# Decayed attention and a Mish layer on one core: state products on quarters of the array, q loaded in runs of eight tokens, two-chunk products

## The chip, the core and the metric

The kernel runs on one core of a Trainium2 chip. A core has five engines that run side by side, each through its own list of instructions in order: PE (TensorE, the 128 x 128 matmul array; its weight loads are shown apart as PEld), DVE (VectorE), ACT (ScalarE), POOL (GpSimd) and SP (SyncE, here a sender of DMAs). Matmul results land in PSUM, which has eight banks of 128 partitions x 512 float32. The metric is the device time of one execution in microseconds (us).

## The reference

```python
# q, k, v: (4 batches, 8 heads, 768 tokens, 64) float32; lam: (8,)
for b in range(nb):                                   # blocks of 64 tokens
    intra = einsum('bhic,bhjc->bhij', qb, kb) * Dmask # lam ** distance, causal
    intra = einsum('bhij,bhjd->bhid', intra, vb)
    inter = einsum('bhid,bhde->bhie', qb * lam_pow, kv_state)
    out[:, :, sl] = intra + inter
    kv_state = lam_block * kv_state + einsum('bhsd,bhse->bhde', kb * rev_pow, vb)
x = out.transpose(0, 2, 1, 3).reshape(3072, 512)
h = x @ w_in                                          # (512, 2048)
g = h * tanh(softplus(h))                             # Mish
return g @ w_out                                      # (2048, 512), float32
```

## The kernel before

Tokens are worked in chunks of 128; a *group* n (0 to 5) is chunk n of all four batches b. All matmuls take float16. For each (group, batch) the kernel takes these steps, each named by a short word:

- `lk`, `lq`, `lv` (L152) load k, q, v from GpSimd's DMA queue, casting to float16, into tiles [token, head, 64]. One contiguous piece is one head of one token, so a load is 1,024 pieces of 256 bytes. k and q of (0,0) come as float32 over the queues of SP and ACT (`fk`, `fq`) and are cast by ACT (`ck`) and VectorE (`cq`, L311).
- Turning: k and q must lie with the 64 channels on the partitions. For groups 0 and 1, PE turns them against the identity (`pk`, `pq`, L316) into a float16 bank; VectorE (`kk`, `eq`) or ACT (`ek`, `ea`, L347) copies the bank to SBUF. For groups 2 to 5 the DMA turns them (`tk`, `tq`). Two heads share the 128 partitions (a pair j of four).
- `sc` (L379): the scores of each head, 8 matmuls on half of the array's rows (64 rows x 128 columns), the two heads of a pair in two banks. `mk` (L385): decay and mask, VectorE, two instructions.
- `yo`, `yt` (L396): scores by v, 8 matmuls of 128 rows x 64 columns. `yi` (L410): the state by q, added in the same bank, 4 matmuls of the full array; the state of a pair is a 128 x 128 tile with the two heads' 64 x 64 parts on the diagonal and zeros beside them. `xd` (L415): VectorE scales the sum into x.
- `kp` (GpSimd) or `kd` (VectorE, L351): decayed k. `pv` (L421): decayed k by v, 4 matmuls of the full array (the off-diagonal parts are computed too). `ra` (L427 for group 0, L430): VectorE adds the old state; `wu` (GpSimd, L434) or `wd` (VectorE, L438) multiplies by the decay `lbm`, which is zero off the diagonal.

Then the Mish layer. The first rows of work go as direct products: `u` (L595), 16 matmuls of 128 columns for 512 hidden units of one chunk, and `mu` (L603), Mish by ACT. They cover all of group 0 and half of group 1. All else uses a scheme of seven half-size products for eight: `p` (L558), 4 matmuls of 256 columns, with sums by VectorE (`ws`, `wt`, `ts`, `gs`, `ad`, `c2`; L455, L458) and copies and Mish by ACT (`ca`, `cc`, `m`; L565, L570, L587). The second layer is the same scheme: `o` (L636), 8 matmuls of 256 columns, copies `oa`, `oc`, `e`, `ed`, and stores `st`.

The order of all this is written out by hand as one string, `ORDER`: a step's name, its numbers (group, batch, ...) and behind `@` its PSUM banks. Each engine meets its instructions in the order of this string; an instruction waits until its operands are there and its bank or tile is free. `zz.N` (L296) are N products of zeros by zeros, 128 columns each, whose result is never read; before the change there are 56 in all, all ahead of the first scores.

Of the kernel before, what the change touches and what calls it, by code (L numbers as in the profile page):

```python
# [7 lines left out]
F32 = mybir.dt.float32  # L8
# [7 lines left out]
fk lq.0.1 ir lk.0.1 lk.0.2 lq.0.2 lv.0.0 lv.0.2 lk.1.2 lq.0.3 lv.0.1 lk.0.3 lk.1.0 la ll z0 zz.23@0 pl@1 an ik  # L16
ak fq ck dk di zz.12@0 pq.0.1@2 eq.0.1 zz.10@0 pk.0.1@3 ie kk.0.1 dv.1 zz.11@0 sc.0.1@2,3 mk.0.1.1 pk.0.2@4
pk.0.0@5 wi.1 wi.0 lv.0.3 lq.1.1 kp.0.0 pq.0.2@6 dv.0 kd.0.1 kk.0.0 mk.0.1.0 dp lz kk.0.2 dq kd.0.2 kp.0.3
lq.1.2 lq.1.0 lk.1.1 wi.3 cq ea.0.2 al pq.0.0@6 ea.0.0 ai lm sc.0.2@5,4 mk.0.2.0 mk.0.2.1 yo.0.1@7 sc.0.0@6,1
pv.0.1@3 pk.1.0@2 pq.0.3@5 ek.1.0 ea.0.3 mk.0.0.0 pk.0.3@4 ek.0.3 yo.0.2@6 pv.0.2@2 mk.0.0.1 xd.0.1 xd.0.2  # L20
yo.0.0@1 pk.1.2@5 sc.0.3@4,7 xd.0.0 mk.0.3.0 mk.0.3.1 pv.0.0@6 u.0.1.2@1 ra.0.2 ra.0.1 u.0.1.1@4 u.0.0.0@7
yo.0.3@2 u.0.0.2@3 mu.0.0.2 mu.0.0.0 xd.0.3 ra.0.0 mu.0.1.2 mu.0.1.1 u.0.0.1@2 u.0.0.3@6 pv.0.3@3 ra.0.3
mu.0.0.3 kk.1.2 mu.0.0.1 u.0.1.3@7 mu.0.1.3 wi.2 kd.1.2 lk.1.3 lq.1.3 pq.1.0@1 pk.1.1@4 pq.1.2@5 pq.1.1@6
lv.1.1 kk.1.1 lv.1.0 lv.1.2 ea.1.0 ea.1.1 eq.1.2 u.0.1.0@3 mu.0.1.0 sc.1.0@4,1 sc.1.2@5,6 sc.1.1@2,7 mk.1.0.0
mk.1.1.0 mk.1.1.1 ws.1.1 mk.1.0.1 mk.1.2.0 kd.1.1 mk.1.2.1 u.0.3.0@3 u.0.3.1@4 u.0.3.2@2 mu.0.3.0 mu.0.3.1
u.0.2.0@7 u.0.3.3@3 u.0.2.2@4 pk.1.3@1 pq.1.3@5 mu.0.2.0 mu.0.3.3 mu.0.2.2 mu.0.3.2 u.0.2.1@7 eq.1.3 kk.1.3
ws.2.1 pv.1.1@5 ra.1.1 lv.1.3 sc.1.3@1,6 yt.1.1@3 yt.1.0@4 u.0.2.3@2 yi.1.1 yi.1.0 yt.1.2@5 mk.1.3.0 mk.1.3.1
# [24 lines left out]
mk.3.1.0 mk.3.1.1 gs.2.1.2.4 gs.2.1.4.6 gs.2.1.6.8 ra.3.0 ra.3.1 gs.2.2.0.2 gs.2.2.4.6 gs.2.2.6.8 p.2.3.4
# [49 lines left out]
def kernel(  # L102
# [10 lines left out]
    nc = tc.nc  # L113
# [661 lines left out]
```

## Time and profile before

| | us |
|---|---|
| median of 3 runs (lowest, highest) | 202.05 (200.88, 228.25) |
| the profiled execution | 202.03 |
| its span, first to last instruction | 200.3 |
| PE busy, PE weight loads | 187.9, 165.5 |
| VectorE busy | 163.4 |
| ACT busy, GpSimd busy | 93.4, 94.4 |
| mean granted PE clock | 0.972 |

The busy times belong to the profiled execution, and so do all rows shown below. A row of groups has line, engine, operation, output <- inputs, shapes and count, then the busy time and the mean in ns, then the idle time ahead of them and what ended it. The chain of waits is read from the end of the execution back: each piece is start, length, engine and line.

### The profile page before, as it was taken

The page shows a single profiled execution, that of the slowest core. Times are in us where ns is not written, and L with a number is a line of the kernel's source. Part 1 is how long each engine was busy: PE and PEld are TensorE (multiplying, and loading weights), DVE is VectorE, ACT ScalarE, POOL GpSimd, SP SyncE. Part 2 cuts the span into 40 slices and gives each one's busy share as a digit, 9 for nine tenths or more (in the row PEclk, how much of TensorE's full clock was granted, in tenths as well). Part 3 has the DMA queues.
Part 4 walks back from the last instruction along what each step waited for, and adds up shares of the span by engine and source line. Part 5 has one row for each costly group of instructions (what it writes and reads, how often), then busy time and mean ns, then how long its engine had stood idle before and what let it go on. Part 6 is the DMA issues. An engine that isn't in the chain of part 4 may idle for free.

```text
span 200.3 us, 5347 instructions
## 1 busy us (share of the span) xinstructions
PE 187.9 (94%) x2226; PEld 165.5 (83%) x2226; DVE 163.4 (82%) x307; ACT 93.4 (47%) x172; POOL 94.4 (47%) x105
## 2 busy tenths in 40 slices
PE   8607999999999999999999999999999999999992
PEld 7406899999899888888888998888988888888882
DVE  2797848799999999999999897879858997788611
ACT  3026166418626231068933448721676526873221
POOL 7999675830518670009994099970094000000000
PEclk9965899999999999999999999999999999999998
DMA  6999999999998949345899646999979331000324
GB/s 82 160 157 206 163 198 163 205 202 157 117 121 107 139 36 236 85 95 50 124 159 152 121 93 150 139 154 195 119 128 85 109 104 54 5 0 0 108 95 167
DMA packets 103226, 24.73 MB, mean 123 GB/s; under 512 B 92834, under 2 KB 103202, under 8 KB 103202
## 3 DMA queue, kind: packets, MB, share of 16 engines
q0 software_dynamic: 77024, 13.37, 85.3%
q1 hardware_dynamic: 24992, 10.69, 24.4%
q10 hardware_dynamic: 1186, 0.33, 0.8%
q8 instruction: 17, 0.28, 0.5%
q14 instruction: 7, 0.06, 0.1%
HBM read 27.26 MB, written 6.29 MB: 168 GB/s over the span
## 4 chain that ended last, share of the span: by engine, by line
PE 86%; DVE 7%; DMA 2%; ACT 2%; issue 1%; POOL 1%; POOLq 0%; DVEq 0%
PE b L636 37%; PE b L558 26%; PE b L595 9%; PE b L396 4%; PE b L379 4%; PE b L410 2%; PE b L421 2%; DMA kn<-in_k_dram 2%; PE b L316 2%; DVE qn L311 1%; ACT hsg L603 1%; DVE ws L458 1%; DVE sb L385 1%; DVE dv L260 1%; DVE ktil L351 1%
## 5 line engine op out<-in xcount | busy, mean ns | idle before, releaser
L636 PEld LDWEIGHTS <-hs 128*128 128x128 f16 x384 | 36.9, 98 | 4.5
L636 PE MATMUL b<-wt,hs 128*128 128x256 f16 x288 | 36.5, 273 | 0.0
L587 ACT ACTIVATE hsg<-b 128x512 f16<-128x512 f32 x54 | 30.0, 598 | 11.6 <-PE b L558 10.5
L385 DVE TENSOR_TENSOR sb<-b,dv 128x512 f16<-128x512 f32 x48 | 30.9, 683 | 3.3 <-PE b L379 2.0
L558 PEld LDWEIGHTS <-ws 128*128 128x128 f16 x288 | 27.7, 98 | 3.6 <-DVE ws L458 0.4
L636 PEld LDWEIGHTS <-hsg 128*128 128x128 f16 x288 | 27.7, 98 | 3.5
L558 PE MATMUL b<-xs,ws 128*128 128x256 f16 x216 | 29.3, 273 | 0.0
L434 POOL TENSOR_TENSOR w<-raw,lbm 128x512 f16<-128x512 f32 x9 | 12.0, 1347 | 32.8 <-DVE raw L430 32.8
L636 PE MATMUL b<-wout,hsg 128*128 128x256 f16 x192 | 24.9, 273 | 0.0
L595 PE MATMUL b<-xt,win 128*128 128x128 f16 x384 | 23.8, 219 | 0.0
L558 PEld LDWEIGHTS <-win 128*128 128x128 f16 x216 | 20.7, 98 | 2.7 <-issue 0.3
L152 POOL DMA_DIRECT2D qn<-in_q_dram x23 | 21.3, 933 | 2.9 <-DMA wout<-in_moe_w_out_dram 1.4
L595 PEld LDWEIGHTS <-win 128*128 128x128 f16 x384 | 22.1, 98 | 0.4
L152 POOL DMA_DIRECT2D kn<-in_k_dram x23 | 20.8, 926 | 3.3 <-DMA wout<-in_moe_w_out_dram 1.7
L351 POOL TENSOR_TENSOR ktil<-kn,lkt 128x512 f16<-128x512 f16 x13 | 14.7, 1137 | 14.9 <-DMA kn<-in_k_dram 14.9
L152 POOL DMA_DIRECT2D vn<-in_v_dram x24 | 21.7, 917 | 0.0
L558 PE MATMUL b<-xt,win 128*128 128x256 f16 x144 | 20.5, 273 | 0.0
L603 ACT ACTIVATE hsg<-b 128x512 f16<-128x512 f32 x24 | 13.3, 604 | 12.9 <-PE b L595 12.9
L565 ACT ACTIVATE b<-b 128x512 f32<-128x512 f32 x18 | 10.5, 590 | 17.9 <-PE b L558 17.2
L415 DVE TENSOR_TENSOR xt<-b,lqi 128x512 f16<-128x512 f32 x24 | 15.8, 686 | 3.2 <-PE b L396 1.7
L455 DVE TENSOR_TENSOR c<-b,p 128x512 f32<-128x512 f32 x18 | 12.3, 685 | 4.2 <-PE b L558 4.2
L455 DVE TENSOR_TENSOR b<-b,p 128x512 f32<-128x512 f32 x18 | 12.5, 697 | 3.4 <-PE b L558 1.7
(77 smaller groups left out, 282.7 us busy)
## 6 DMA issues: line engine op xcount, KB each, us to landing
out_dram<-osb SPq DMA_DIRECT2D x23, 256.0 KB, 2.5
vn<-in_v_dram POOLq DMA_DIRECT2D x24, 128.0 KB, 6.0
qn<-in_q_dram POOLq DMA_DIRECT2D x23, 128.0 KB, 5.8
kn<-in_k_dram POOLq DMA_DIRECT2D x23, 128.0 KB, 5.8
win<-in_moe_w_in_dram POOLq DMA_DIRECT2D x4, 512.0 KB, 9.5
wout<-in_moe_w_out_dram POOLq DMA_DIRECT2D x4, 512.0 KB, 10.4
osb<-in_k_dram SPq DMA_DIRECT2D x1, 256.0 KB, 3.0
osb<-in_q_dram ACTq DMA_DIRECT2D x1, 256.0 KB, 5.5
```

The costliest lines, as they stand in the source:

```text
L152: nc.gpsimd.dma_start(out=to[n, b], in_=rows(t, n, b))
L351: engine.tensor_tensor(out=ktil[n, b], in0=kn[n, b], in1=bc(lkt, 2, D), op=ALU.mult)
L385: nc.vector.tensor_tensor(out=sb[n, b, t], in0=pS[n, b][t], in1=dv[:, t], op=ALU.mult)
L415: nc.vector.tensor_tensor(out=xts(n, b), in0=pO.pop((n, b)), in1=lqi, op=ALU.mult)
L434: nc.gpsimd.tensor_tensor(out=wst[b], in0=raw.pop((n, b)), in1=lbm, op=ALU.mult)
L455: nc.vector.tensor_tensor(out=o, in0=a, in1=b, op=ALU.add)
L558: nc.tensor.matmul(t[:, mi, :], w_half(i, s, mi, kc), x_half(n, i, kc), start=(i in (1, 5) and mi == 0 and kc == 0), stop=(mi == 1 and kc ...
L565: nc.scalar.activation(ph[n, s, "b"], ph[n, s, "a"], AF.Copy)
L587: nc.scalar.activation(hidden(n, col - 1, row - 1)[:, 2 * s : 2 * s + 2], src, AF.Mish)
L595: nc.tensor.matmul(ph[n, w, b][:, f, :], win[:, kc, ni * 128 : (ni + 1) * 128], xt[n][:, kc, b * C : (b + 1) * C], start=(f == 0 and kc == ...
L603: nc.scalar.activation(hidden(n, b // 2, w // 2)[:, f : f + 4, cols], ph.pop((n, w, b)), AF.Mish)
L636: nc.tensor.matmul(t[:, tb, :], g_half(n, i, ki, tb), o_half(i, ki), start=(i in (1, 5) and tb == 0 and ki == 0), stop=(tb == 1 and ki == ...
```

## The change

1. **State on quarters.** The state of a pair is now 128 x 64: the two heads' 64 x 64 parts one below the other, without zeros. `pv` becomes 8 matmuls of 128 rows x 64 columns with 64 moving columns; `yi` becomes 8 matmuls on the diagonal quarters (64 x 64) of the array; `ra`, `wu`, `wd` work on 128 x 256 elements instead of 128 x 512. `sc` also goes on quarters: 16 matmuls of 64 x 64 instead of 8 of 64 x 128. The step `lz` (clearing `lbm`) goes.
2. **q of groups 0 and 1 in runs of 8 tokens.** A partition holds 8 tokens of one head, so a load is 128 pieces of 2 KB. PE turns it by 16 matmuls against parts of the identity (64 columns each) into a float32 bank, and the copy to SBUF puts the tokens back in order.
3. **Two-chunk products.** 20 of the 24 `u` steps become `uu`: 8 matmuls of 256 columns for 256 hidden units of two chunks; 20 `mu` become `mv`.
4. **Wide zero products.** `zz` takes 512 columns per matmul; the counts are now 12, 20, 5, 124, 2 and 2 in units of 128 columns (165 in all).
5. **Tiles and order.** Eight instead of seven buffers each for k, q and v. The whole `ORDER` is new: among other things three more k are copied by ACT and not by VectorE (`ek` 5, `kk` 3), five more k are decayed by GpSimd (`kp` 18, `kd` 2), q is copied by ACT seven times and once by VectorE, 14 loads (of groups 0 and 1) stand ahead of the first slice of w_in instead of 11 ahead of its slices 1 and 0, and steps of like shape stand in groups (three or four `sc`, four `yi`).

```diff
 ORDER = """
-fk lq.0.1 ir lk.0.1 lk.0.2 lq.0.2 lv.0.0 lv.0.2 lk.1.2 lq.0.3 lv.0.1 lk.0.3 lk.1.0 la ll z0 zz.23@0 pl@1 an ik
-ak fq ck dk di zz.12@0 pq.0.1@2 eq.0.1 zz.10@0 pk.0.1@3 ie kk.0.1 dv.1 zz.11@0 sc.0.1@2,3 mk.0.1.1 pk.0.2@4
...
+fk ir lk.0.1 lq.1.2 lq.0.2 lk.0.2 lv.0.1 lk.0.3 lk.1.0 lq.1.3 lq.0.3 lq.1.0 lq.0.1 lk.1.2 lv.0.0 lq.1.1 ll fq
+la ck z0 zz.12@0 pl@1 ik di cq dk zz.20@0 pk.0.0@2 zz.5@0 pq.0.0@3 pk.0.1@4 zz.124@0 pq.0.1@5 an ek.0.1 ak
+kd.0.2 kk.0.0 dv.0 dp eq.0.0 ie dq dv.1 sc.0.0@1,4 mk.0.0.0 ai ea.0.1 al wi.0 lv.0.2 mk.0.0.1 pk.1.0@2
+pk.0.2@3 pk.0.3@6 ek.1.0 ek.0.3 sc.0.1@5,7 ek.0.2 mk.0.1.1 mk.0.1.0 pq.0.3@1 pq.0.2@4 pq.1.3@2 yo.0.0@6 xd.0.0
+ea.0.3 ea.0.2 pk.1.2@7 ek.1.2 zz.2@0 yo.0.1@3 xd.0.1 pq.1.0@5 pq.1.1@1 ea.1.0 sc.0.3@6,4 zz.2@0 sc.0.2@3,7
+ea.1.1 uu.0.0.0.0@5 mk.0.2.0 uu.0.0.0.1@1 mk.0.3.1 mk.0.2.1 mk.0.3.0 lv.0.3 wi.2 wi.3 lk.1.1 lk.1.3 lv.1.0
+kp.0.0 wi.1 pv.0.0@3 yo.0.2@4 pq.1.2@7 lm ea.1.3 mv.0.0.0.0 mv.0.0.0.1 ea.1.2 xd.0.2 pv.0.2@2 yo.0.3@6
...
+    def runs(t, n, b):
+        return t[b, :, n * C : (n + 1) * C, :].rearrange("h (g r) c -> h g r c", r=RUN)
...
     def lq(n, b):
-        load(qn, q, "qn", n, b)
+        if n > 1:
+            load(qn, q, "qn", n, b)
+            return
+        qn[n, b] = work.tile([128, H, D], F16, name="qn", tag="qn", bufs=8)
+        nc.gpsimd.dma_start(out=qn[n, b], in_=runs(q, n, b))
...
-        t = bank(at, [128, 4 * C])
-        for _ in range(m):
-            nc.tensor.matmul(t[:, 0:128], kzero, kzero, start=True, stop=True)
+        t = bank(at, [128, 4, C])
+        for n in [4] * (m // 4) + [1] * (m % 4):
+            nc.tensor.matmul(t[:, 0:n], kzero, bc(kzero, 1, n), start=True, stop=True)
...
     def pq_(n, b, at):
-        pq[n, b] = turn_by_pe(qn[n, b], at)
+        o = pq[n, b] = bank(at, [128, RUN, JP, C // RUN])
+        pick = ident.rearrange("p (j t g) -> p t j g", t=2, g=C // RUN)
+        for r in range(RUN):
+            for t in range(2):
+                nc.tensor.matmul(o[part[t], r], qn[n, b][:, r, :], pick[:, t], start=(r == 0), stop=(r == RUN - 1))
+
+    def q_copy(copy, n, b):
+        src = pq.pop((n, b))
+        copy(turned(qraw, "qraw", n, b).rearrange("p j (g r) -> p r j g", r=RUN), src)
...
         for j in range(JP):
-            for t in range(2):
-                nc.tensor.matmul(pS[n, b][t][:, j, :], kraw[n, b][part[t], j, :],
-                                 qraw[n, b][part[t], j, :], start=(j == 0), stop=(j == JP - 1))
+            for x in range(2):
+                for t in range(2):
+                    nc.tensor.matmul(pS[n, b][t][part[x], j, :], kraw[n, b][part[t], j, part[x]],
+                                     qraw[n, b][part[t], j, :], start=(j == 0), stop=(j == JP - 1))
...
     def yi(n, b):
         for j in range(JP):
-            nc.tensor.matmul(pO[n, b][:, j, :], wst[b][:, j, :], qraw[n, b][:, j, :],
-                             start=False, stop=(j == JP - 1), skip_group_check=True)
+            for t in range(2):
+                nc.tensor.matmul(pO[n, b][part[t], j, :], wst[b][part[t], j, :], qraw[n, b][part[t], j, :],
+                                 start=False, stop=(j == JP - 1), skip_group_check=True)
...
     def pv_(n, b, at):
-        o = pv[n, b] = bank(at, [128, JP, C])
+        o = pv[n, b] = bank(at, [128, JP, D])
         for j in range(JP):
-            nc.tensor.matmul(o[:, j, :], flat(ktil[n, b])[:, j * C : (j + 1) * C],
-                             flat(vn[n, b])[:, j * C : (j + 1) * C], start=(j == 0), stop=(j == JP - 1))
+            for t in range(2):
+                nc.tensor.matmul(o[part[t], j, :], ktil[n, b][:, 2 * j + t, :], vn[n, b][:, 2 * j + t, :],
+                                 start=(j == 0), stop=(j == JP - 1))
...
+    def uu(n, w, h, f0, at):
+        ph[n, w, h, f0] = bank(at, [128, 2, HT])
+        for f in range(2):
+            ni = 4 * w + 2 * f0 + f
+            for kc in range(NKC):
+                nc.tensor.matmul(ph[n, w, h, f0][:, f, :], win[:, kc, ni * 128 : (ni + 1) * 128],
+                                 xt[n][:, kc, h * HT : (h + 1) * HT],
+                                 start=(f == 0 and kc == 0), stop=(f == 1 and kc == NKC - 1))
```

More of the change, by code (lines that the diff above doesn't have):

```diff
@@ L150, in load @@
     def load(to, t, name, n, b):
-        to[n, b] = work.tile([128, H, D], F16, name=name, tag=name, bufs=7)
+        to[n, b] = work.tile([128, H, D], F16, name=name, tag=name, bufs=8)
         nc.gpsimd.dma_start(out=to[n, b], in_=rows(t, n, b))
@@ L173, in fq @@
         f32["q"] = work.tile([128, H, D], F32, name="osb", tag="osb", bufs=4)
-        nc.scalar.dma_start(out=f32["q"], in_=rows(q, 0, 0))
+        nc.scalar.dma_start(out=f32["q"], in_=runs(q, 0, 0))
     @step
@@ L202 @@
     lqi = const.tile([128, JP, C], F32, name="lqi")
-    lbm = const.tile([128, JP, C], F32, name="lbm")
+    lbm = const.tile([128, JP, D], F32, name="lbm")
     kzero = const.tile([128, C], F16, name="kzero")
@@ L270, in lz @@
     @step
-    def lz():
-        nc.vector.memset(lbm, 0.0)
-    @step
     def al():
-        for t in range(2):
-            rs = slice(64 * t, 64 * t + 64)
-            nc.scalar.activation(lbm[rs, :, rs], bc(lnp[rs], 2, D), AF.Exp, scale=float(C))
+        nc.scalar.activation(lbm, bc(lnp, 2, D), AF.Exp, scale=float(C))
     @step
@@ L304, in ck @@
     def ck():
-        kn[0, 0] = work.tile([128, H, D], F16, name="kn", tag="kn", bufs=7)
+        kn[0, 0] = work.tile([128, H, D], F16, name="kn", tag="kn", bufs=8)
         nc.scalar.activation(kn[0, 0], f32["k"], AF.Copy)
@@ L309, in cq @@
     def cq():
-        qn[0, 0] = work.tile([128, H, D], F16, name="qn", tag="qn", bufs=7)
+        qn[0, 0] = work.tile([128, H, D], F16, name="qn", tag="qn", bufs=8)
         nc.vector.tensor_copy(qn[0, 0], f32["q"])
+    part = [slice(0, 64), slice(64, 128)]
     def turn_by_pe(src, at):
@@ L342, in eq_ @@
     def eq_(n, b):
-        nc.vector.tensor_copy(turned(qraw, "qraw", n, b), pq.pop((n, b)))
+        q_copy(nc.vector.tensor_copy, n, b)
     @step
     def ea(n, b):
-        nc.scalar.activation(turned(qraw, "qraw", n, b), pq.pop((n, b)), AF.Copy)
+        q_copy(lambda o, x: nc.scalar.activation(o, x, AF.Copy), n, b)
     def decayed(engine, n, b):
@@ L370, in tq @@
         nc.sync.dma_start_transpose(out=turned(qraw, "qraw", n, b), in_=flat(qn[n, b]))
-    part = [slice(0, 64), slice(64, 128)]
     @step
@@ L428, in ra @@
             return
-        raw[n, b] = work.tile([128, JP, C], F32, name="raw", tag="raw", bufs=3)
+        raw[n, b] = work.tile([128, JP, D], F32, name="raw", tag="raw", bufs=3)
         nc.vector.tensor_tensor(out=raw[n, b], in0=pv.pop((n, b)), in1=wst[b], op=ALU.add)
```

154 lines of the change are left out of this document (78 added, 76 removed).

## The prediction, on record before the result

> **What bounds the kernel now.** I read first the busy shares and the slices of the page, then the same busy times over four stretches, which I cut where TensorE's (PE's) work changes its kind.
>
> ```profile
> PE 187.9 (94%) x2226; PEld 165.5 (83%) x2226; DVE 163.4 (82%) x307; ACT 93.4 (47%) x172; POOL 94.4 (47%) x105
> ...
> PEclk9965899999999999999999999999999999999998
> ...
> GB/s 82 160 157 206 163 198 163 205 202 157 117 121 107 139 36 236 85 95 50 124 159 152 121 93 150 139 154 195 119 128 85 109 104 54 5 0 0 108 95 167
> ```
> ```profile
> 0.00:6.00 6.00, 4.63 (x46) 4.24 (x47) 1.12 (x7) 2.39 (x4) 4.86 (x10) 1.00 0.88 88
> 6.00:16.00 10.00, 2.85 (x44) 2.05 (x41) 9.50 (x16) 1.43 (x3) 9.93 (x13) 0.77 2.13 167
> 16.00:22.60 6.60, 6.54 (x80) 4.84 (x81) 4.53 (x9) 4.09 (x6) 5.06 (x6) 0.57 1.69 186
> 22.60:197.00 174.40, 173.85 (x2064) 154.37 (x2061) 148.23 (x278) 85.19 (x158) 74.56 (x78) 1.00 1.05 120
> ```
>
> The columns are the stretch, its length, the busy time of PE, PE's weight loads, DVE (VectorE), ACT (ScalarE) and POOL (GpSimd), the granted clock, DMA share and GB/s. From 22.6 us on PE is busy 173.85 of 174.40 us: there only less PE work helps. Before it PE does 5.6 us of useful work (the turns, scores and states ahead of the first direct product, priced below) in 22.6 us, 6.54 us of its time at a granted clock of 0.57. After the last product at 197 us come 3.3 us of copies and stores. So the end is start of the dense stream + its work + tail, and the change can move the first two. The chain of waits shows what sets the start.
>
> ```profile
> 2.59 4.19 DMA kn<-in_k_dram
> ...
> 13.82 2.19 DVE qn L311
> 16.02 0.05 issue
> 16.06 0.61 PE b L316 x4
> ...
> 20.14 0.57 PE b L396 x8
> ...
> 22.80 2.68 PE b L595 x48
> ```
> ```profile
> PE b L316 <- DVE qn L311: 5.5, 1, 5.5
> ```
>
> VectorE does a row of small constants, then the cast of q (L311), and PE stands still 5.5 us for it. Then all goes at half clock: intra (L396) takes 0.57 us for 8 matmuls, later 0.34 (below).
>
> **The dense stream, term by term.** The same chain prices each kind of matmul at full clock.
>
> ```profile
> 54.40 0.87 PE b L636 x8
> ...
> 57.45 0.22 PE b L421 x4
> 57.68 0.89 PE b L595 x16
> ...
> 72.77 0.33 PE b L379 x8
> 73.10 3.60 PE b L636 x32
> ...
> 76.70 0.34 PE b L396 x8
> 77.04 0.55 PE b L379 x16
> ...
> 77.93 1.75 PE b L636 x16
> ...
> 82.30 0.79 PE b L396 x24
> 83.09 0.55 PE b L410 x8
> ```
>
> A 256-column matmul costs 0.109 us (0.87/8), one of 128 columns 0.0556 (0.89/16), so each further 128 columns 0.0535. Scores (64 rows x 128 columns of the array) cost 0.22 per 8: 0.55 less 0.33. Intra (128 x 64) costs 0.028 per matmul, from (0.79 - 0.34)/16. Both run two at a time. What stays over is a change of the array's shape: 0.33 - 0.22 = 0.11 us going in, and 3.60 - 32 x 0.109 = 0.11 going out.
>
> *Two-chunk products (uu).* 20 of 24 direct steps change from 16 matmuls of 128 columns (0.89) to 8 of 256 (0.87): -0.02 x 20 = **-0.35 us**. They need both chunks of a half, so the first one needs two finished x tiles.
>
> ```profile
> L396 PEld LDWEIGHTS <-vn 128*64 128x64 f16 x192 | 6.2, 115 | 2.3 <-issue 1.2 <-DVE hs L455 0.2 <-DMA win<-in_moe_w_in_dram 0.2
> L421 PEld LDWEIGHTS <-ktil 128*128 128x128 f16 x80 | 5.9, 101 | 0.9 <-issue 0.4
> ```
>
> *State update (pv, 20 steps).* Four matmuls, 0.22, become eight of 64 columns on 128 x 64. By the slope a 64-column matmul costs 0.029, pairs run together as intra does: 4 x 0.029 = 0.12, -0.106 x 20 = **-2.1**. From both sides: nothing gained if the eight weight loads (115 ns each in intra's rows against 98 for full ones) set the pace at 0.028 each, +0.22 x 20 = +4.5 if none pair. I take the row of intra, the nearest.
>
> *Inter (yi, 20 steps) and scores (sc, 24 steps) on quarters.* Inter becomes eight matmuls, two quarters at a time: 4 x 0.056 = 0.22, what four cost now. Scores become sixteen: at four at a time 0.22, as now; at two at a time 0.45, +0.22 x 24 = +5.4. No row has a quarter. Two halves run at once by rows (L379) and by columns (L396), and I take four at once: **0** for both; a gain is excluded, since each quarter still takes 128 columns through the array and no more than four quarters exist. The other end stays a rival.
>
> *Changes of shape.* I counted them in the two written orders: 54 before, 59 after; from the first direct product on, 42 and 46 (pv and inter now differ in shape from the products, but the new order puts pv beside intra and inter beside scores). 4 x 0.11 = **+0.4**.
>
> The Trainium skill, TensorEngine Tiling (Array Packing), section Key Properties, says that changing the tiling mode drains the engine, which speaks against a change that adds modes. The page gives no price; the 0.11 us above is that drain as this trace has it, and by it the rule costs the 0.4 us already in the sum.
>
> Sum of the dense stream: -0.35 - 2.1 + 0 + 0.4 = **-2.0**; useful work ahead of it stays about 5.5 us, since what pv gains there goes into other turns.
>
> *VectorE and GpSimd beside it.* State tiles halve.
>
> ```profile
> L351 POOL TENSOR_TENSOR ktil<-kn,lkt 128x512 f16<-128x512 f16 x13 | 14.7, 1137 | 14.9 <-DMA kn<-in_k_dram 14.9
> L434 POOL TENSOR_TENSOR w<-raw,lbm 128x512 f16<-128x512 f32 x9 | 12.0, 1347 | 32.8 <-DVE raw L430 32.8
> L430 DVE TENSOR_TENSOR raw<-b,w 128x512 f32<-128x512 f32 x16 | 10.9, 683 | 0.5 <-PE b L421 0.4
> L351 DVE TENSOR_TENSOR ktil<-kn,lkt 128x512 f16<-128x512 f16 x7 | 4.8, 682 | 0.0
> L455 DVE TENSOR_TENSOR b<-b,q 128x256 f32<-128x256 f32 x2 | 0.9, 432 | 1.2 <-ACT q L654 1.1
> ```
>
> Twenty state reads (L427, L430) and seven updates (L438) go from 683 ns to about 430 (the row of a 128 x 256 add), 27 x 0.25 = 6.8 us; five decays of k move to GpSimd (5 x 0.68 off VectorE, 5 x 1.14 on GpSimd, whose nine updates (L434, 1347 ns) shrink by up to half). VectorE's 148 us in a stretch of 174 was no bound; it falls by about 12 and that is worth **0**, except in the dense stretch's own stalls of 0.55 us.
>
> **The start.** Queue issues first, for GpSimd sends nearly all loads.
>
> ```profile
> 9.57 1.82 POOL L152 DMA_DIRECT2D kn<-in_k_dram  x2
> ...
> 11.30 1.59 POOL L178 DMA_DIRECT2D win<-in_moe_w_in_dram  x2
> ```
> ```profile
> 5.53 0.40 PE L316 MATMUL b<-ident,qn 128*128 128x128 f16 x4 [0.38 <-DMA qn<-in_q_dram]
> ```
>
> A load of 1,024 pieces costs GpSimd 0.91 us to issue, a weight load of 512 pieces 0.80; by that slope a q in runs of 8 tokens (128 pieces) costs about 0.7. Landing is the slower side: slices of the GB/s row that carry loads stand at 157 to 163, those of weights at 198 to 206. So 128 KB takes 0.83 us in short pieces, 512 KB of w_in 2.56, and a q in runs, pieced like weights, 0.64. The first k was usable at 6.8 us, third in its queue, the first q at about 5.5.
>
> The new queue (group, batch) is k (0,1), q (1,2), q (0,2), k (0,2), v (0,1), k (0,3), k (1,0), q (1,3), q (0,3), q (1,0), q (0,1), k (1,2), v (0,0), q (1,1), w_in slice 0. The first lands at about 5.6 us. Up to q (0,1) lie four short-piece loads and six in runs: 4 x 0.83 + 6 x 0.64 = 7.2, so **12.8 to 13.8 us** (the span takes the float32 q on ACT's queue in). Slice 0 of w_in comes after two more loads and one in runs, 2.3, plus 2.56: **17.7 to 18.7**.
>
> ```profile
> 0.99 2.37 PEld L296 LDWEIGHTS <-kzero 128*128 128x128 f16 x23 [0.99 <-DVE kzero L238]
> ```
>
> PE's zero products fill this time: 124 blocks of 128 columns as 31 matmuls of 0.216 (0.0556 + 3 x 0.0535) are 6.7 us, behind about 6.5 us of earlier zeros and turns: until about 13.2, when q (0,1) lands, so nothing waits for them at full clock. The 56 narrow zeros of before left PE idle from 6 to 16 us, and the clock fell for it.
>
> ```profile
> L385 DVE TENSOR_TENSOR sb<-b,dv 128x512 f16<-128x512 f32 x48 | 30.9, 683 | 3.3 <-PE b L379 2.0
> L415 DVE TENSOR_TENSOR xt<-b,lqi 128x512 f16<-128x512 f32 x24 | 15.8, 686 | 3.2 <-PE b L396 1.7
> L565 ACT ACTIVATE b<-b 128x512 f32<-128x512 f32 x18 | 10.5, 590 | 17.9 <-PE b L558 17.2 <-ACT q L654 0.5
> L347 ACT ACTIVATE qraw<-b 128x512 f16<-128x512 f16 x5 | 2.9, 612 | 8.8 <-PE b L316 8.8
> ```
>
> From q (0,1): its turn, the copy by ACT (0.6), scores, two masks on VectorE, behind two masks of batch 0 (4 x 0.68), intra, two scalings (2 x 0.69): 13.4 + 0.3 + 0.6 + 0.4 + 2.7 + 0.3 + 0.7 = 18.4. On ACT ten copies of 0.6 stand from the same point up to the one that frees the first product's bank (q (1,0)): 13.6 + about 5.5 = 19.1. The q copies now read float32 (596 to 612 ns per copy either way, as the rows have it) and write in steps of 8; if that doubles them, four of the ten cost 2.4 us more, and at nothing they cost 0. First direct product: **about 19.2**, against 22.7. Behind it pv (0,0) needs a k decayed on GpSimd, queued behind six more issues, and the x tiles of batches 2 and 3 need VectorE's masks: about **1 us** of waits before the stream is dense. Net **-2.5 us**; between -3.5 (no waits) and 0 (ACT's chain 2.4 later).
>
> **Sum.** Span 200.3 - 2.0 - 2.5 = 195.8; the profiled execution took 202.03, 1.73 more than its span: 197.5. The median shown, 202.05, is the same as that execution, so the forecast is 2.2% under it. The tail's steps stay. 2% (198.0 below, 206.1 above) is about what a measurement tells from no change.
>
> **Rivals.**
> 1. *The start isn't earlier.* ACT's and VectorE's chains, or waits behind the first product, take the 2.5 us back, and the dense stream alone counts: 202.0 - 2.0 = **200.0**. For it: ten ACT copies now stand between one late q and the first product. Against: VectorE's cast no longer stands there.
> 2. *Inter's two quarters take turns.* Both write one bank. The cost is +0.22 x 20 = 4.5: **202.0**, no change. For it: in scores now, the two row halves write two banks, never one. Against: they write different partitions, as intra's halves do in one bank without loss. The Trainium skill, TensorEngine Tiling (Array Packing), section Gotcha 1: PSUM Pressure, says that different row tiles cannot access the same bank at the same time. By that rule inter would go as in this rival; no row of before has row halves in one bank, so the trace doesn't decide.
> 3. *Slower: row halves never overlap on quarters.* Scores at two at a time (+5.4) and inter one at a time (+4.5): 197.5 + 9.9 = **207.4**. One mechanism, in 44 steps; it cancels the gain from +0.1 us per step (4.5/44) and makes the kernel slower by 2% from (206.1 - 197.5)/44 = 0.2 per step. Against it: L379's halves overlap now.
> 4. *The change doesn't hold the clock.* If the long zeros run at half clock (2.37/23 = 0.103 per 128 columns as at the start, so 31 x 4 x 0.103 = 12.8 us), q (0,1) is turned at 19.5 instead of 13.4: +6: **203.5**.
>
> **How the numbers follow.** Forecast 0.55 (its own range 195 to 199.5; 0.46 of it below 198.0), rival 1 0.2 (a little of it under 198.0), rival 2 0.08, rival 3 0.08, rival 4 0.09 (half clock longer still would pass 206). Faster 0.48, same 0.41, slower 0.11. The range runs from 194.5 (-3.5 at the start, 0.5 of stalls gone) to 202.5, which takes in rivals 1 and 2 and leaves out 3, 4 and a little below.
>
> **What would show it.** First direct product at 18.5 to 20 us and PE dense soon after it; granted clock near 1.00 from 6 to 22 us; two scores in a row 0.22 us apart; pv at 0.12 per step and inter at 0.22; VectorE near 150 us; PE near 100% from the first product on for about 172 us. Wrong, if scores or inter cost twice that, if the clock falls between 13 and 20 us, or if the new order, in which inter, masks and copies stand in other places, opens new stalls in the dense stretch; I see none, but each of 60 groups could hide one.

## The result, and the profile after

The changed kernel takes 214.26 us (median of 4 runs, 213.83 to 215.2) against 202.03 for the kernel before (4 runs beside it): a ratio of 1.063, with a 95% interval of 1.057 to 1.069. (Ratios, here and below, leave out executions in the slower state that any kernel here falls into now and then; one of the four before took 228.25 us.) That is outside the forecast range and on the other side. The profiled execution has a span of 213.4 us, 13.1 more than before.

The page of the changed kernel, its busy shares and three of its slices, and then the same cuts in time as were shown of before, with the stretch after 22.6 us cut finer (stretch, length, PE, weight loads, VectorE, ACT, GpSimd, granted clock, DMA share, GB/s):

```profile
PE 197.6 (93%) x2503; PEld 165.0 (77%) x2503; DVE 150.9 (71%) x295; ACT 106.9 (50%) x177; POOL 92.9 (44%) x110
...
PE   8696674999999999999999999999999999999993
...
PEclk9997858599999999999999999999999999999999
```
```profile
0.00:6.00 6.00, 4.67 (x16) 1.84 (x16) 0.59 (x5) 1.98 (x3) 5.10 (x11) 1.00 0.71 105
6.00:16.00 10.00, 8.29 (x85) 4.20 (x86) 6.74 (x11) 1.00 (x3) 8.93 (x13) 1.00 1.84 167
16.00:22.60 6.60, 4.55 (x114) 3.90 (x114) 3.68 (x7) 6.60 (x8) 6.20 (x8) 0.74 1.56 192
22.60:30.00 7.40, 3.85 (x62) 2.46 (x58) 3.02 (x5) 7.40 (x5) 6.86 (x8) 0.69 1.65 189
30.00:40.00 10.00, 6.70 (x99) 4.66 (x99) 4.20 (x8) 7.08 (x6) 6.98 (x8) 0.67 1.64 188
40.00:60.00 20.00, 20.00 (x312) 17.57 (x310) 10.90 (x21) 7.60 (x14) 6.05 (x7) 0.94 1.00 109
60.00:190.00 130.00, 129.57 (x1645) 112.74 (x1643) 111.53 (x219) 66.25 (x124) 52.78 (x59) 1.00 1.07 107
```

Up to 16 us the zero products hold the clock at 1.00, as forecast; q (0,1), which was to land by 13.8 us, is turned at 15.18, behind a wait for its load. From 16 to 40 us PE is busy 15.1 of 24 us, the clock falls to about 0.7, and ACT has no idle time between 16 and 30 us. From 40 us on PE has no gap to speak of, only a clock that is back at 1.00 from 44 us (0.94 in the stretch to 60). So nearly all that was lost was lost before 40 us. The chain of waits (start, length, engine, line) names the work that ACT and VectorE did in it; the two groups behind it are the copies of q, from the page and from the answer on the tile qraw:

```profile
12.27 2.44 DVE qraw L343
...
16.42 2.33 ACT qraw L363
...
20.41 4.64 ACT qraw L363 x2
25.05 0.42 ACT kraw L351
25.47 4.61 ACT qraw L363 x2
...
34.77 2.35 ACT qraw L363
```
```profile
L363 ACT ACTIVATE qraw<-b 128x512 f16<-128x512 f32 x7 | 16.9, 2563 | 0.0
```
```profile
L363 ACT ACTIVATE qraw<-b x7: 2422/2472/2816, 16.3 to 34.6; 128x512 f16<-128x512 f32 x7
...
L343 DVE CAST qraw<-b x1: 2437/2437/2437, 12.3 to 12.3; 128x512 f16<-128x512 f32 x1
```

A copy of q that puts the tokens in order takes 2.4 to 2.8 us on ACT and 2.44 on VectorE. Before, ACT's copies of q took 0.61 and VectorE's 0.42:

```profile
L343 DVE COPY qraw<-b 128x512 f16<-128x512 f16 x3 | 1.3, 422 | 3.6 <-PE b L316 3.6
```

PE waits for them; the timeline of PE shows the turn of q (0,1) and the first direct product, which before began at 22.63 us:

```profile
15.18 0.44 PE L339 MATMUL b<-ident,qn 128*64 128x64 f16 x16 [0.26 <-DMA qn<-in_q_dram]
...
27.85 1.86 PE L629 MATMUL b<-xt,win 128*128 128x256 f16 x8 [1.44 <-ACT qraw L363]
30.13 1.87 PE L629 MATMUL b<-xt,win 128*128 128x256 f16 x8 [0.41 <-ACT qraw L363]
...
33.91 0.32 PE L438 MATMUL b<-vn,ktil 128*64 128x64 f16 x8 [1.05 <-ACT qraw L363]
...
37.16 0.64 PE L394 MATMUL b<-qraw,kraw 64*64 64x128 f16 x16 [1.93 <-ACT qraw L363]
37.73 2.53 PE L629 MATMUL b<-xt,win 128*128 128x256 f16 x11
```

The stream is dense only from 37.7 us, behind the last of these copies.

The prices of the dense stream came out as forecast. The same chain, later, at full clock:

```profile
113.00 0.79 PE b L394 x48
113.80 5.35 PE b L669 x48
...
119.84 0.12 PE b L438 x8
...
121.99 1.01 PE b L426 x32
...
170.00 0.57 PE b L394 x32
...
176.98 0.56 PE b L426 x16
```

L394 is sc: 16 more matmuls cost 0.79 - 0.57 = 0.22 us, so four quarters run at once. L426 is yi: 16 more cost 1.01 - 0.56 = 0.45, or 0.22 per step of eight, so two quarters run at once in one bank. L438 is pv: 0.12 per step. The change of shape costs 0.79 - 3 x 0.22 = 0.13 going in and 5.35 - 48 x 0.109 = 0.12 going out here; before it was 0.11.

### The profile page after: what moved, and what is told of

Its sections match the earlier page's. It is cut to its first block, busy times and chain, and to the rows that moved or that the text cites. A ratio compares the mean times of both kernels' runs of the same rounds, so it can differ in the third digit from the quotient of the medians.

```text
span 213.4 us, 5897 instructions
## 1 busy us (share of the span) xinstructions
PE 197.6 (93%) x2503; PEld 165.0 (77%) x2503; DVE 150.9 (71%) x295; ACT 106.9 (50%) x177; POOL 92.9 (44%) x110
## 4 chain that ended last, share of the span: by engine, by line
PE 71%; DVE 12%; ACT 10%; DMA 3%; issue 1%; POOL 1%; DVEq 0%; POOLq 0%
PE b L669 30%; PE b L575 25%; ACT qraw L363 7%; PE b L629 6%; DMA kn<-in_k_dram 3%; DVE hs L475 3%; PE b L394 2%; PE b L411 2%; PE b L426 2%; DVE sb L400 2%; PE b L612 1%; DVE xt L431 1%; DVE qraw L343 1%; PE b L438 1%; ACT kraw L351 1%
## 5 line engine op out<-in xcount | busy, mean ns | idle before, releaser
L604 ACT ACTIVATE hsg<-b 128x512 f16<-128x512 f32 x54 | 30.1, 600 | 9.5 <-PE b L575 9.2
L367 POOL TENSOR_TENSOR ktil<-kn,lkt 128x512 f16<-128x512 f16 x18 | 19.6, 1096 | 22.4 <-PE b L438 13.7
L451 POOL TENSOR_TENSOR w<-raw,lbm 128x256 f16<-128x256 f32 x9 | 7.2, 807 | 43.8 <-DVE raw L447 33.4
L629 PE MATMUL b<-xt,win 128*128 128x256 f16 x160 | 23.1, 307 | 1.9 <-ACT qraw L363 1.9
L575 PEld LDWEIGHTS <-win 128*128 128x128 f16 x216 | 21.0, 98 | 2.6
L629 PEld LDWEIGHTS <-win 128*128 128x128 f16 x160 | 17.4, 110 | 6.0 <-issue 2.4
L575 PE MATMUL b<-xt,win 128*128 128x256 f16 x144 | 20.5, 273 | 0.0
L709 ACT ACTIVATE osb<-b 128x512 f32<-128x512 f32 x12 | 7.2, 598 | 21.7 <-PE b L669 21.7
L363 ACT ACTIVATE qraw<-b 128x512 f16<-128x512 f32 x7 | 16.9, 2563 | 0.0
L636 ACT ACTIVATE hsg<-b 128x512 f16<-128x512 f32 x20 | 11.2, 618 | 11.0 <-PE b L629 11.0
```

What stands on the lines that cost most here:

```text
L363: q_copy(lambda o, x: nc.scalar.activation(o, x, AF.Copy), n, b)
L367: engine.tensor_tensor(out=ktil[n, b], in0=kn[n, b], in1=bc(lkt, 2, D), op=ALU.mult)
L575: nc.tensor.matmul(t[:, mi, :], w_half(i, s, mi, kc), x_half(n, i, kc), start=(i in (1, 5) and mi == 0 and kc == 0), stop=(mi == 1 and kc ...
L604: nc.scalar.activation(hidden(n, col - 1, row - 1)[:, 2 * s : 2 * s + 2], src, AF.Mish)
L629: nc.tensor.matmul(ph[n, w, h, f0][:, f, :], win[:, kc, ni * 128 : (ni + 1) * 128], xt[n][:, kc, h * HT : (h + 1) * HT], start=(f == 0 and ...
L636: nc.scalar.activation(hidden(n, h, w // 2)[:, f : f + 2], ph.pop((n, w, h, f0)), AF.Mish)
```

## The experiments

The expectations give each theory a letter. The main one (A): the copies of q cost four times what was assumed since they write in steps, and this alone made the start late. Against it stood that any copy that reorders is slow (B), that the new order, with ten copies on ACT between one late q and the first product, was at fault (C), and that the quarters or their shape changes were.

**The copy writes in one piece.** PSUM is read in steps instead; both ends keep the same tokens.

```diff
-        copy(turned(qraw, "qraw", n, b).rearrange("p j (g r) -> p r j g", r=RUN), src)
+        copy(turned(qraw, "qraw", n, b).rearrange("p j (g r) -> p j g r", r=RUN), src.rearrange("p r j g -> p j g r"))
```

> The changed kernel with one edit: the copy of a turned q writes its 512 elements in one piece and steps through PSUM instead (the tokens are put in order on the read side). Theory A (a copy that writes float16 elements 16 bytes apart costs 2.4 to 2.5 us instead of 0.6, and eight of them hold up the start): the copies cost 0.6 to 0.75 us, the first direct product comes at 19 to 22 us instead of 27.9, PE is dense soon after, and the time is 198 to 201 us. Rival B (any reordering copy is slow, whichever side steps): the copies stay near 2.4 us and the time near 214. Rival C (the start is long for other reasons: the chain of ten ACT copies, waits on masks, the clock): the copies cost 0.6 us but the time stays above 204.

Measured: 204.05 us (203.66 to 204.18), ratio to before 1.014 (1.005 to 1.024). From the groups of this kernel:

```profile
L363 ACT ACTIVATE qraw<-b 128x512 f16<-128x512 f32 x7 | 4.1, 610 | 3.3 <-PE b L339 3.3
...
L343 DVE CAST qraw<-b 128x512 f16<-128x512 f32 x1 | 0.7, 692 | 0.0
```

A copy takes 610 ns on ACT and 692 on VectorE. Reading PSUM with steps of 256 bytes between neighbours costs ACT nothing, and writing SBUF with steps of 16 bytes cost 1.9 us per copy. One line of the kernel is worth 10.2 us. But 204.05 is above the 198 to 201 that were expected, and still behind before: first direct product at 23.7 us, not at the forecast 19.2. So fast copies with a time above 204, as in rival C, is what is seen, and a second cause is left.

**The new order with q as before.** Quarters, two-chunk products, zeros and order are kept; all q come head by head and are turned by four matmuls.

```diff
     def lq(n, b):
-        if n > 1:
-            load(qn, q, "qn", n, b)
-            return
-        qn[n, b] = work.tile([128, H, D], F16, name="qn", tag="qn", bufs=8)
-        nc.gpsimd.dma_start(out=qn[n, b], in_=runs(q, n, b))
+        load(qn, q, "qn", n, b)
...
-        copy(turned(qraw, "qraw", n, b).rearrange("p j (g r) -> p r j g", r=RUN), src)
+        copy(turned(qraw, "qraw", n, b), pq.pop((n, b)))
```

> The changed kernel with q of groups 0 and 1 loaded and turned as before the change (1,024 pieces, turned against the identity into a float16 bank, copied in one piece); order and all else as changed. Theory A: the slow copies are gone, the loads are a little longer (seven times 0.2 us), so 199 to 203 us. Rival B says the same. Rival C: above 207, since order and waits stay.

Measured: 200.73 us (199.63 to 201.7), ratio 0.996 (0.991 to 1.000). The new order is not at fault for the loss. The profile has a span of 198.2; PE's timeline and the chain of waits show its start:

```profile
21.50 1.92 PE L620 MATMUL b<-xt,win 128*128 128x256 f16 x16 [0.96 <-DMA win<-in_moe_w_in_dram]
```
```profile
13.64 7.81 DMA win<-in_moe_w_in_dram
```

With q in short pieces the first product waits for slice 0 of w_in (13.64 + 7.81 = 21.45), which no longer comes sooner by the runs. From the first product to the end of the span it takes 198.2 - 21.5 = 176.7 us, before 200.3 - 22.6 = 177.7: 1.0 less. The forecast had the same sum, -2.0 of work and 1 us of waits behind the first product, but the trace has other parts: from its first product to its last PE is busy 172.98 us and idle 0.15, before 173.82 and 0.29. So the waits didn't come, and PE's work there fell by 0.8 us, not by 2.0. How much of the difference is work that the new order moves across the first product was not taken apart.

**Before's order, quarters alone.** sc, yi and pv on quarters and the small state, nothing else.

```diff
-            nc.tensor.matmul(pO[n, b][:, j, :], wst[b][:, j, :], qraw[n, b][:, j, :],
-                             start=False, stop=(j == JP - 1), skip_group_check=True)
+            for t in range(2):
+                nc.tensor.matmul(pO[n, b][part[t], j, :], wst[b][part[t], j, :], qraw[n, b][part[t], j, :],
+                                 start=False, stop=(j == JP - 1), skip_group_check=True)
```

> The kernel before with only the quarters (state 128 x 64, pv, yi and sc as changed, lz gone), in the old order. By the terms of the prediction: pv gives 2.1 us; but in the old order the array's shape now changes 99 times instead of 54, 87 instead of 42 after the first direct product, 45 x 0.11 = 5.0 us more: 203 to 206 us. A rival in which a change of shape costs only where PE would otherwise be early (it is hidden): 199.5 to 201. If scores or inter took twice as long on quarters: above 208.

Measured: 203.62 us (202.31 to 204.94), ratio 1.015 (1.001 to 1.028). The output of this kernel has a relative error of 0.18, and no run shows why; it prices the steps and is no version to use. In this order the array changes shape 99 times instead of 54, since the state update now has intra's shape and inter has the scores', and neither has that of the products any more. By the row of before, 45 changes more at 0.11 would cost 5.0, less pv's 2.1: 2.9. The median shows 1.1 of it, the trace the whole: from the first product to the last PE is busy 177.01 us instead of 173.82, and the first product comes at 20.0 us instead of 22.6. So in this order the quarters cost more PE time than they save; with like shapes together, and with the two-chunk products (the kernel above), PE's work fell by 0.8 us.

**Before's order, q in runs alone.** The loads of 128 pieces, the turn by 16 matmuls and the copy that writes in steps, in the old order.

```diff
-        nc.vector.tensor_copy(turned(qraw, "qraw", n, b), pq.pop((n, b)))
+        q_copy(nc.vector.tensor_copy, n, b)
```

> The kernel before with only q of groups 0 and 1 in runs of 8 tokens (loads, turns and stepping copies as changed), in the old order. Theory A: the five copies on ACT and three on VectorE cost 2.4 us each instead of 0.4 to 0.6; four of group 0 stand ahead of the first direct product, but the old order has waits there that hide a part: 204 to 210 us. Rival C (the loss comes with the new order): within 1.5 us of 202.

Measured: 213.62 us (212.57 to 216.62), ratio 1.061 (1.045 to 1.076), above what was expected. Its groups:

```profile
L368 ACT ACTIVATE qraw<-b 128x512 f16<-128x512 f32 x5 | 12.1, 2529 | 8.4 <-PE b L344 8.4
L348 DVE CAST qraw<-b 128x512 f16<-128x512 f32 x3 | 7.3, 2435 | 6.4 <-PE b L344 6.4
```

The runs alone, loads, turns and stepped copies, in an order where three of the eight copies stand on VectorE, give the whole loss. The first experiment changed the side of the step and nothing else, and that settles the main cause: the runs put in cost 11 us, and the step taken out of the copies gives 10 back.

**What the price of a step hangs on.** The seven ACT copies each write with another step; tokens of q come out of order, the work is the same.

```diff
+        how = {(0, 0): 8, (0, 1): 1, (0, 3): 2, (0, 2): 4, (1, 0): 8, (1, 1): 16, (1, 3): 32, (1, 2): 0}[n, b]
```

> The changed kernel with the eight copies of turned q writing in different ways, so one look prices the step: batch 0.1 in one piece, 0.3 in steps of 2 elements (4 bytes), 0.2 of 4 (8 bytes), 1.0 and 0.0 of 8 (16 bytes), 1.1 of 16, 1.3 of 32, and 1.2 in pieces of 16 whole elements in permuted order; all read PSUM straight through. It leaves the tokens of q out of order, which changes the scores' values and no shape. Theory A1 (each write that goes to another 16 bytes costs, as the skill's rule on lines of 16 bytes would have it): steps 1, 2, 4 at 0.6 us, steps 8, 16, 32 at about 2.5, permuted pieces 0.6. Theory A2 (any step above one element costs): 2 and 4 are slow too. Theory A3 (short pieces and four-dimensional patterns cost): the permuted pieces are slow and long-run steps of 8 are faster than 2.5.

Measured in one execution (206.92 us): steps of 1, 2, 4, 8, 16, 32 elements of two bytes take 580, 772, 1338, 2487, 2752, 2419 ns on ACT, and whole runs of 16 elements in another order (the entry 0) 599. VectorE with a step of 8 takes 2434. Five of them in ACT's timeline, with steps of 1, 2, 8 and 32, and the whole runs:

```profile
16.39 0.58 ACT L369 ACTIVATE qraw<-b 128x512 f16<-128x512 f32 x1
...
18.61 0.77 ACT L369 ACTIVATE qraw<-b 128x512 f16<-128x512 f32 x1
...
20.80 2.49 ACT L369 ACTIVATE qraw<-b 128x512 f16<-128x512 f32 x1
...
26.80 2.42 ACT L369 ACTIVATE qraw<-b 128x512 f16<-128x512 f32 x1
...
30.01 0.60 ACT L369 ACTIVATE qraw<-b 128x512 f16<-128x512 f32 x1
```

The time goes with the number of times that the write enters a new piece of 16 bytes: 64, 128, 256 and 512 entries for steps 1, 2, 4 and 8, and 512 from there on. From 4 to 8 that is 256 entries for 1.15 us, 4.5 ns each. From 8 on the entries are the same and the times lie within 14%, which the count doesn't explain. Steps of 2 already cost 0.19 us, and of 4 0.76, where theory A1 had them free. The Trainium skill, Advanced Engine Details and Errata, section Memory Cachelines, has SBUF lines of 16 bytes and full performance from two hits on a line. The line size agrees; the threshold doesn't: step 4 has two hits on each line and took 1338 ns, more than twice the whole copy.

**The second cause: loads in 8 groups or in 16.** In the load of runs the outermost count is 8 heads, then 16 runs. Turned round, the same 128 pieces have 16 outermost. The turn picks other columns, the rest is the first experiment.

```diff
-        return t[b, :, n * C : (n + 1) * C, :].rearrange("h (g r) c -> h g r c", r=RUN)
+        return t[b, :, n * C : (n + 1) * C, :].rearrange("h (g r) c -> g h r c", r=RUN)
...
-        pick = ident.rearrange("p (j t g) -> p t j g", t=2, g=C // RUN)
+        pick = ident.rearrange("p (g j t) -> p t g j", t=2, j=JP)
```

> The kernel of e1 (copies write in one piece) with the runs of q spread over the partitions group by group instead of head by head, so that the load's outermost count is 16 and not 8; loads, turns and copies have the same sizes. Theory D (with the outermost count 8 a load in runs goes to half of the 16 DMA engines, so early loads wait behind it): between 4 and 8 us the queues move some 600 short pieces per 0.5 us instead of 150 to 210, k (0,2) lands by 8.5 us instead of 10.1, q (0,1) by 13.5 instead of 15.4, the first direct product comes near 21, and the time falls from 204 to 199 to 201 us. Rival E (pieces of 2 KB are slow to start or block short ones, whatever their order): no change, 203 to 205.

Measured: 201.95 us (201.37 to 204.7), ratio 1.003 (1.000 to 1.006): better than the first experiment's 1.014, and short of the 199 to 201 us of theory D. The two kernels differ in when the loads were there: the first decayed k, behind k (0,2), began at 10.18 us and now begins at 8.77; q (0,1) was turned at 15.45, behind a wait for its load, and is now turned at 14.01, right behind the zero products. The one moved by 1.4 us and the other by at least that, so the early loads behind the runs came that much sooner. The Trainium skill, DMA: Bandwidth & Descriptors, section on why a DMA increments its semaphore by 16, paragraph "How many engines (k)", says that a transfer goes to the largest number of engines up to 16 that divides the slowest count on both of its sides; by that rule 8 heads outermost use 8 engines of 16. The direction agrees; the profile has no engine numbers, so the mechanism is not shown.

The rest of this kernel's delay stands in three stalls for which the profile finds no releaser. PE's timeline:

```profile
20.24 0.28 PE L339 MATMUL b<-ident,qn 128*64 128x64 f16 x6 [1.93 <-issue]
...
21.37 1.92 PE L629 MATMUL b<-xt,win 128*128 128x256 f16 x16
...
26.43 0.31 PE L394 MATMUL b<-qraw,kraw 64*64 64x128 f16 x8 [1.33 <-issue]
```

The first cuts one turn of q in two, between two matmuls with the same inputs: no data can be late there. Counted in the trace, PE's instructions 449, 705 and 1217 are those behind the three stalls (2.12, 1.54 and 1.05 us from the start of one instruction to that of the next): 193 plus a multiple of 256. In the first experiment's kernel the stalls stand at 449 and 1217 alone (2.51 and 0.79). The queues section of the page has, for before and for this kernel, in that order:

```profile
q8 instruction: 17, 0.28, 0.5%
```
```profile
q8 instruction: 19, 0.31, 0.6%
```

17 and 19 packets of 16 KB, one for each 256 of PE's some 4,480 and 5,030 instructions; one of them starts at 17.78 us, 0.34 before the first stall, another at 23.82 before the second. Before, 449 was reached at 25.8 us, without a stall. The Trainium skill, Runtime: NRT & Kernel Launch, section Instruction fetch mechanics, has blocks of 256 instructions, fetched by DMA and mostly hidden. The blocks agree; here three were not hidden.

The traces of all thirteen kernels together say more than these two packets. PE never passes 449, or a later one of these counts, sooner than 1.24 us after the packet of the same number in that queue (the first for 449, the second for 705, and so on) has ended. At 13 of 234 such counts PE stands idle for over 0.3 us, and each of these stalls ends 1.24 to 1.72 us behind its packet: here 18.75, 24.72 and 40.71 for the packets' ends, 20.24, 26.43 and 42.20 for PE's going on.

**The long zeros.** The new order with q as before, without the 124 zero products ahead of q (0,1).

```diff
-la ck z0 zz.12@0 pl@1 ik di cq dk zz.20@0 pk.0.0@2 zz.5@0 pq.0.0@3 pk.0.1@4 zz.124@0 pq.0.1@5 an ek.0.1 ak
+la ck z0 zz.12@0 pl@1 ik di cq dk zz.20@0 pk.0.0@2 zz.5@0 pq.0.0@3 pk.0.1@4 pq.0.1@5 an ek.0.1 ak
```

> The kernel of e2 without the 124 blocks of zero products ahead of q (0,1). Theory F (the zeros hold the clock while PE waits for loads): the granted clock is 0.5 from about 12 to 20 us; five us of useful PE work ahead of the first products take up to twice as long, and the time rises by 1 to 3.5 us over e2's 200.7, to 202 to 204. Rival G (the start waits for loads and VectorE anyway, so the clock there is worth nothing): 200 to 201.5.

Measured: 201.35 us (201.12 to 202.79) against 200.73 with them, ratios 1.001 (0.998 to 1.005) and 0.996 (0.991 to 1.000). Its stretches:

```profile
6.00:16.00 10.00, 1.34 (x20) 0.97 (x24) 4.50 (x11) 1.49 (x4) 10.00 (x12) 0.60 2.91 146
16.00:22.60 6.60, 6.60 (x103) 5.13 (x98) 3.96 (x6) 4.72 (x10) 6.60 (x9) 0.57 1.76 185
```

Without the zeros the clock is at 0.60 and 0.57, with them at 1.00 in both stretches. First direct product at 23.1 instead of 21.5 us. The clock is held as forecast, and 201.35 lies in rival G's range: the zeros are worth about 0.6 us by the medians and 1.1 by the ratios, and the intervals overlap, so that they are worth anything isn't clear of the noise.

**Where PE's blocks of instructions end.** Two kernels with nothing changed but the number of PE instructions ahead: part of the long zeros, or all of them, go in 128 columns each instead of 512, so that the work stays and the instructions behind move along.

```diff
-... zz.124@0 pq.0.1@5 ...
+... zz.60@0 zn.64@0 pq.0.1@5 ...      # 48 matmuls more, 96 instructions with their weight loads
+... zn.124@0 pq.0.1@5 ...             # the other kernel: 93 matmuls, 186 instructions
```

> The kernel of e6 with the 124 blocks of zero products issued as 15 matmuls of 512 columns and 64 of 128 instead of 31 of 512: the same columns, 96 PE instructions more, all ahead of q (0,1). In e1 and e6 PE stood still in the middle of a step, waiting for nothing the profile shows, before its instructions number 449, 705 and 1217 (all 193 + a multiple of 256), 4.7 us in all in e6. Theory H (PE's instructions come in blocks of 256 by DMA, and there PE has used up a block before the next is in): the stalls move or go, since the same steps now lie 96 instructions earlier in their block; a block ends at what was instruction 353 and is asked for while the zeros run; stalls before 25 us fall from 3.7 us to under 1.5 and the time from 201.95 to 198 to 200.5 us. Rival I (the stall belongs to the steps themselves, to their banks or loads): it stays at the same two steps (the turn of q (1,1), the scores of (1,2)), time 201.5 to 203.

> The kernel of e6 with the 124 blocks of zero products as 124 matmuls of 128 columns: 186 PE instructions more ahead of q (0,1), the same columns. Theory H: block ends fall on what were instructions 263 and 519, the second after a dense stretch; stalls of up to 1.5 us there, time 199 to 201.5 us. Rival I: as in e6, 201.5 to 203. If narrow zeros cost more time (0.0556 against 0.054 per 128 columns) that is 0.2 us.

Measured: with 96 more 200.03 us (199.21 to 201.92), ratio 0.994 (0.989 to 0.998); with 186 more 202.45 (200.33 to 203.83), ratio 0.999 (0.995 to 1.002), profiled in an execution of 203.83 us. The second time lies in rival I's range and not in H's; what speaks for H is where the stalls stand. With 96 more, 449 and 1217 pass without a stall, the first direct product comes at 19.8 us (the forecast had 19.2), and one stall is left:

```profile
19.80 1.92 PE L636 MATMUL b<-xt,win 128*128 128x256 f16 x16
...
23.33 0.32 PE L346 MATMUL b<-ident,qn 128*64 128x64 f16 x8 [0.98 <-issue]
```

It stands at instruction 705 again (1.17 us), though 705 is now in a turn of q and was in scores. With 186 more it is at 705 once more (2.58 us, at 19.54). The stall goes with the count, not with the work; theory H had it there in the second kernel, with at most 1.5 us.

**66 more.** 80 blocks of 128 columns of zeros in wide matmuls and 44 in narrow ones, instead of 60 and 64.

> The kernel of e8 with a smaller shift: 20 zero products of 512 columns and 44 of 128 (66 PE instructions more than e6 instead of 96). Theory H: block ends fall on what were instructions 383 and 639 of e6; the second is met some 0.7 us later than in e8, when its block may be in: the stall of 1.2 us at instruction 705 shrinks, another of up to 0.5 us may open at 449; time 199 to 200.5 us.

Measured: 200.55 us (199.59 to 202.32), ratio 0.994 (0.991 to 0.998).

```profile
18.72 0.41 PE L418 MATMUL b<-sb,vn 128*64 128x128 f16 x7 [0.78 <-issue]
...
24.65 0.22 PE L445 MATMUL b<-vn,ktil 128*64 128x64 f16 x1 [1.38 <-issue]
```

The stalls are at 449 and 705 (1.02 and 1.58 us), now in yo and in the last matmul of a pv. That the one at 705 would shrink was wrong: where a block's end falls decides, and by how much I could not foretell. The packets tell it afterwards: they end at 17.45 and 23.31 us, and PE goes on at 18.72 and 24.65.

**Fewer PE instructions.** The kernel with 96 more, and the scores of groups 0 and 1 on halves as before the change: 64 matmuls, 128 instructions fewer, and the same time of the array (0.22 us per sc either way).

```diff
     def sc(n, b, ...):
+        if n < 2:
+            for j in range(JP):
+                for t in range(2):
+                    nc.tensor.matmul(pS[n, b][t][:, j, :], kraw[n, b][part[t], j, :],
+                                     qraw[n, b][part[t], j, :], start=(j == 0), stop=(j == JP - 1))
+            return
```

> The kernel of e8 with the scores of groups 0 and 1 on halves of the array as before the change (8 matmuls instead of 16, the same 0.22 us): 128 PE instructions fewer before about 34 us, and up to six changes of shape more (0.1 us each) where scores stand beside inter. Theory H: fewer instructions per microsecond in the start, so the stall at 22 us goes and the time is 198.5 to 200 us. Rival I (the number of instructions does not matter): no gain, 200 to 201 us.

Measured: 198.58 us (198.34 to 199.26), ratio 0.985 (0.980 to 0.991). This is the best version, ahead of the kernel before and of the change. Its stretches up to 22.6 us and its first direct product:

```profile
6.00:16.00 10.00, 9.61 (x145) 7.03 (x143) 6.26 (x13) 2.60 (x6) 9.60 (x15) 1.00 1.83 175
16.00:22.60 6.60, 6.60 (x195) 5.48 (x191) 5.91 (x11) 6.57 (x13) 5.83 (x7) 1.00 1.55 193
```
```profile
19.49 1.92 PE L642 MATMUL b<-xt,win 128*128 128x256 f16 x16
...
23.87 0.40 PE L401 MATMUL b<-qraw,kraw 64*128 64x128 f16 x8 [0.94 <-ACT qraw L370]
```

PE is busy without a gap from 16 to 22.6 us, at full clock. The time is as expected, the way to it isn't: 705 still has a gap of 1.15 us. An ACT copy that ended at 23.00 stands in its first third, and the profile names it, but PE goes on only at 23.87, 1.59 us behind the end of the packet, as in the other stalls. The profiles of this kernel and of the one it was made from, the latter of its fastest execution, differ by 0.3 us in span, the medians by 1.45, so what the halves gave is measured but not seen in the traces.

## Why the prediction was wrong, step by step

- **The step that failed** is the last term of the start: "The q copies now read float32 (596 to 612 ns per copy either way, as the rows have it) and write in steps of 8; if that doubles them, four of the ten cost 2.4 us more, and at nothing they cost 0". The chain around it was right, the size wasn't. A stepped copy measured 2.43 to 2.56 us on average, on ACT 4.2 times the old one, and the doubling that I took as the far end was picked from no row. Four of them stand on ACT ahead of the first product, 4 x 1.9 = 7.6 us: 19.2 + 7.6 = 26.8, measured 27.85. The other three follow while PE waits for them, up to 37.7. No row of before showed a stepped write, and so no row gave its cost an upper end.
- **The loads.** 0.64 us per q in runs, pieced like weights, left out the order of the counts: with heads outermost the early loads came 1.4 us later than with runs outermost. At 16 outermost, q (0,1) was turned at 14.01, right behind the zero products, just past the 12.8 to 13.8 forecast for its landing; when it landed doesn't show.
- **PE's instructions.** Not foreseen. The change makes the start's work out of more and smaller instructions, and PE reached the ends of blocks before it could go on past them, which it never did sooner than 1.24 us behind a packet's end.
- **The first direct product at 19.2**: 19.5 and 19.8 us in the last kernels, once these three are out. The shape of the start was right.
- **The dense stream, -2.0**: right in its prices, not shown in its sum. sc and yi cost what they did (0.22), pv 0.12, the changes of shape about 0.12 against 0.11, VectorE fell from 163.4 to 150.9, as forecast; no run tried what that is worth alone. But PE's busy time from the first product to the last fell only from 173.8 to 173.0 us, in the order with q as before, and to 173.1 in the last kernel.
- **The clock**: held by the long zeros as forecast, and worth some 0.6 to 1.1 us by itself, not clear of the noise. After's fall to 0.7 from 16 to 40 us goes with PE's waits: with the copies written whole it was 0.98 and 0.91 in the stretches from 16 and from 22.6 to 40 us.
- **The rivals.** Rival 1 (ACT's chain takes the start back) named the engine, and capped its price at the gain. Rivals 2 and 3 fall by the rows of L394 and L426. By the rule of the Trainium skill, TensorEngine Tiling (Array Packing), section Gotcha 1: PSUM Pressure, that different row tiles cannot access one bank at the same time, yi would take an estimated 0.45 per step; the trace shows 0.22, two row tiles in one bank at different partitions. Rival 4 falls by the granted clock of 1.00 up to 16 us. No rival had slower by a stepped write.

Where the way from the change to the forecast 197.5 went, by the ratios of the kernels that follow each other, each times 202.05 (214.8 for the change, 17.3 us above the forecast): the stepped copies 1.063 to 1.014, 9.9 us; the loads to 1.003, 2.2; the instruction blocks to 0.994 by moving them, 1.9; and to 0.985 in the kernel with fewer instructions, 1.7. About 1.6 us stays open; the last kernel still has a gap of 1.15 at 705, and its dense stream isn't 2.0 us shorter in work. The last two terms rest on intervals about 2 us wide, and were measured beside other runs of before.

## What to carry to other kernels

A copy that changes the order of elements should do so on the side that it reads from PSUM and write SBUF in whole runs; the other way round it cost four times as much on ACT (2.56 us against 0.61) and 3.5 times on VectorE (2.44 against 0.69). An operation with an access pattern that no row of the profile has gets a range as wide as the worst plausible count (here one access for each line of 16 bytes), not a doubling, above all where several of them stand in the one chain that sets the start. When work is cut into smaller matmuls, count PE's instructions as well as their columns: in a busy start the blocks of 256 can come late. A stall with no releaser in the middle of one step is how that looks, and the end of the packet in the instruction queue, 1.2 to 1.7 us ahead of PE's going on, tells it from other waits.

## What the runs showed of the hardware

- ACT writes f16 from a float32 bank to SBUF in 580 to 610 ns per 128 x 512 when whole, in 772, 1338, 2487 ns at steps of 2, 4, 8 elements, and in 2752 and 2419 at 16 and 32; read steps in PSUM were free (610 ns). VectorE takes 692 ns whole, read in steps, and 2434 at a write step of 8.
- Four 64 x 64 quarters run at once (16 matmuls of 128 columns in 0.22 us), and two of them can write one bank at different partitions without loss of time (8 matmuls in 0.22 us).
- One packet of 16 KB comes in the instruction queue for each 256 instructions of PE, and gaps of up to 2.6 us stood exactly at 193 + 256 x k in eight kernels, on other instructions of the work; each ended 1.24 to 1.72 us behind its packet, and at none of 234 such counts did PE go on sooner. That the fetch is their cause is inferred from this; no run could take the fetch away.
- 128 pieces of 2 KB came sooner with 16 than with 8 as the outermost count of the load.
